# A gated mix of two attentions, forward and backward: preparation reordered, output projection of the first attention back in a stage of its own

## The chip, the core and the metric

The kernel runs on one core of a Trainium2 chip. The metric is device time in microseconds from start to end of one execution; the median of the runs is given. The engines are TensorE (PE, with its weight loads as PEld), VectorE (DVE), ScalarE (ACT), GpSimd (POOL) and SyncE (SP). SP and POOL issue nearly all DMAs.

## The reference

Inputs are bf16. The forward function and its vector-Jacobian product for 11 inputs are computed, so the kernel writes twelve outputs: the result and eleven gradients. With 2048 tokens and model width 576:

```python
g = _sigmoid((x * gate_w).sum(-1, keepdims=True))
a = _A_ref(x, A_wq, A_wk, A_wv, A_wo)      # 32 heads of 18, one shared k and v, no mask
b = _B_ref(x, B_mem0, B_Wq, B_Wk, B_Wv, B_Wo, 32)
return g * a + (1 - g) * b

def _B_ref(x, mem0, Wq, Wk, Wv, Wo, seg_len):   # 32 heads of 128
    mem = mem0                                   # 8 memory rows
    for s in range(64):                          # segments of 32 tokens
        h = concatenate([mem, xs])               # 40 rows
        q, k, v = projections of h
        p = softmax(where(mask, q k / sqrt(128), -1e9))
        o = (p v) Wo
        mem = o[:, :8]                           # carried to the next segment
        outs.append(o[:, 8:])
```

The memory rows make the second attention (B) a recurrence of 64 steps, forward and backward. The first (A) has no recurrence.

## The kernel before, in words

`build_full` (L1630) runs one stage after another; each opens pools of SBUF and PSUM memory, stacked in the order of the `with` lines, and the next stage's pools take the same addresses.

- Preparation: `prep` (L1173) loads x and grad_out, computes the gate g, transposes x into xT, makes g times grad_out (daT, da_dram) and (1-g) times grad_out (dbT, db_dram). `a_weights` (L1227) loads and lays out the weights of A, `a_setup` (L1265) makes k and v of A. `a_qd_all` (L1318) computes, in 16 head pairs times 4 blocks of 512 tokens, the transposed q and gradient products of A (`a_qd`, L1323): ten matmuls into one PSUM tile a_pq, their absolute values on ACT, one more matmul with a_smneg that adds a bound for the softmax, a copy by DVE, a store. `zero_fill` (L112) writes zeros to pq_dram (16 stores of 512 KB) and to the padding of otok_dram.
- Projections of B: `load_Wo`, `make_WoT` (L448) transposes Wo on PE; `b_proj_x` (L183) projects the 16 token tiles of dbT with WoT (dO). It also carries `stash_WT` (L177), 48 pieces: a transposing DMA of a piece of Wq, Wk or Wv into one of two p_wt buffers (SP), and its store to st_WT (POOL). Then `load_W` (L160) loads Wk, Wq and Wv (4.7 MB each), and `b_proj_x` projects five tiles of x with Wk, Wv and Wq; the other tokens' rows ride along in the chain.
- Forward chain: `b_chain_fwd` (L235), 64 segments, woven piece by piece (`weave`) with `a_pass1` (L1339), the forward softmax of A. Each segment also writes its heads' outputs, as oTm_dram and, copied into another order by POOL, as oh_dram (`head_out`). `a_pass1` ends with 128 small stores of a_dlT on SP. A's outputs go to otok_dram (L1456).
- Bulk stage: `b_bulk` (L473) does all token rows of attention B, forward and the larger part of backward, in 128 steps of four heads. Its ten to thirteen stage functions are called in a hand-written order (L697), each on another step, as a software pipeline: q, k and dO transposes, scores and exponentials (st_S), row sums and normalised P (st_R), transposes of P (st_T), output (st_O), its transposes (st_OT), gradient of the scores (st_D), b (st_B), transposes of dS (st_DT), dq (st_Q), memory gradients (st_K). Six of them share two PSUM buffers, x_tr.
- Backward chain (`b_chain_bwd`, woven with `a_pass2`), `b_post` (L930), and the weight gradients `b_dw` (L1042): 16 pieces of matmul groups, beside them the memory tokens of dq, dk and dv (`mem_tok`, L417), and per piece one tile of the gate (`gate_load`, `gate`, L720 to 754). `gate` does the output projection of A there: a transposing DMA of otok_dram, ten matmuls with w_wo, then the mix with b. For the memory rows of "o", `b_dw` reads oh_dram with transposing DMAs (L1057).
- `a_final` (L1556): the remaining gradients of A.

What orders the work: the four woven or pipelined stages stand under `manual_schedule`, where every engine's and queue's order is the program's. All other stages are ordered at compile time by the framework's planner, which takes any instruction whose inputs and memory are free in its own model of time, the earlier in the program first. [...]

Of the kernel before, what the change touches and what calls it, by code (L numbers as in the profile page):

```python
# [11 lines left out]
P = 128  # L12

D = 576
# [16 lines left out]
class Kern:  # L31
# [52 lines left out]
    def setup_B_dram(self, dram):  # L84
# [5 lines left out]
        self.da_dram = t("da_dram", [T, D])  # L90
        self.dxB_dram = t("dxB_dram", [T, D])
# [7 lines left out]
        self.oh_dram = t("oh_dram", [NSEG // 16, E, HB, P])  # L99
# [11 lines left out]

    def zero_fill(self, sp):  # L112
        nc = self.nc
        z = sp.tile([P, 16, P], BF16, name="zfill")
        nc.gpsimd.memset(z[:], 0.0)
        for tt in range(self.NTT):
            nc.gpsimd.dma_start(self.pq_dram[tt].rearrange("s q c w k -> (s q c) w k"), z[:])
        nc.gpsimd.dma_start(self.otok_dram[:, D:NKT * P].rearrange("(n p) d -> p n d", p=P), z[:, 0:self.NTT, 0:64])
# [41 lines left out]
    def load_W(self, pool):  # L160
        nc = self.nc
        self.W = {}
        for w, src in (("k", self.B_Wk), ("q", self.B_Wq), ("v", self.B_Wv)):
            t = pool.tile([P, NKT, J], BF16, name="W" + w)
            nc.vector.memset(t[64:128, 4, :], 0.0)
            for kt in range(NKT):
                rows = KT_ROWS[kt]
                self.dq_eng().dma_start(t[0:rows, kt, :], src[kt * P:kt * P + rows, :])
            self.W[w] = t
# [65 lines left out]
    def b_chain_fwd(self, keep, sp, psum):  # L235
# [33 lines left out]
        for s in range(NSEG):  # L269
# [8 lines left out]
            def head_out():  # L278
                c0 = 8 * (s % 16)
                nc.sync.dma_start(self.oh_dram[s // 16][:, :, c0:c0 + 8], oh[:].rearrange("p c u q -> p (c u) q"))  # L280

# [18 lines left out]
            for j in range(2):  # L300
                proj("k", j)
                if j == 0 and s + 1 < NSEG:
                    load_ride(s + 1)
                yield
# [54 lines left out]
            oh = sp.tile([P, 4, 8, 8], BF16, name="c_oh", bufs=1)  # L359
            nc.gpsimd.tensor_copy(oh[:], oT[:].rearrange("p u c q -> p c u q"))  # L360
            yield
            if s + 1 < NSEG:
# [13 lines left out]
                head_out()  # L376
# [18 lines left out]
            else:  # L395
                yield
                head_out()
# [19 lines left out]
    def mem_tok(self, wi, sp, psum, nb):  # L417
        nc = self.nc

        def load(mt):  # L420
            src = sp.tile([P, 16, 256], BF16, name="z_src", bufs=2)
            nc.sync.dma_start(src[:], self.dTm_dram[mt][:, wi])
# [50 lines left out]
    def b_bulk(self, wp, sp, psum):  # L473
# [76 lines left out]
        def transp(x, m, nm):  # L550
# [3 lines left out]
            self.tr(pt[:, 4, :], m.rearrange("p i t -> p (i t)"), P)  # L554
# [14 lines left out]
        def trans(t, w, nb):  # L569
            tt, g, r, d = view(t)  # L570
            pt = psum.tile([P, 5, P], BF16, name="x_tr", bufs=2)
            for i in range(4):
                self.tr(pt[:, i, :], d[w][:, 4 * (g % 4) + i, :], P)
            o = sp.tile([P, 4, P], BF16, name=f"x_{w}T", bufs=nb)
            self.evac(o[:], pt[:, 0:4, :], use="s" if w == "dO" else "v")
            sc[w + "T", t] = o

        st_QT = lambda t: trans(t, "q", 2)
        st_KT = lambda t: trans(t, "k", 2)
        st_GT = lambda t: trans(t, "dO", 6)  # L580

        def st_S(t):
# [13 lines left out]
            sc["E", t] = Et  # L596

        def st_R(t):
            tt, g, r, d = view(t)
            Et = sc.pop(("E", t))  # L600
# [80 lines left out]
        def st_K(t):  # L681
# [9 lines left out]
            if t % 4 == 3:  # L691
                c2 = t // 4 % 2
                for i in range(4):
# [3 lines left out]
        order = [(0, st_QT), (1, st_S), (2, st_T), (3, st_O), (0, st_KT), (1, st_R), (4, st_OT), (5, st_D), (0, st_GT),  # L697
                 (6, st_B), (7, st_DT), (8, st_Q), (6, st_K)]
        issue = (st_O, st_D, st_K, st_Q)
        with self.tc.manual_schedule():  # L700
# [8 lines left out]
            for t in range(NG + 8):  # L709
                for n, st in order:  # L710
                    if 0 <= t - n < NG:
                        st(t - n)
                    if st in issue and n in after and t - n >= 0 and (t - n) % 4 == 3:
# [6 lines left out]
    def gate_load(self, tt, sp):  # L720
        r = slice(tt * P, (tt + 1) * P)
        L = []
        for nm, src, dt in (("o_b", self.b_dram, F32), ("o_go", self.grad_out, BF16)):
# [3 lines left out]
        t = sp.tile([P, NKT, P], BF16, name="o_T", bufs=1)  # L727
        self.nc.sync.dma_start_transpose(t[:], self.otok_dram[r, :])
        L.append(t)
        return L  # L730

    def gate(self, tt, L, wo, sp, psum):
        nc = self.nc
        bsb, go, oT = L
        diff = sp.tile([P, D], F32, name="o_diff", bufs=1)
        pa = [psum.tile([P, 512], F32, name="w_acc", bufs=6) for _ in range(2)]
        for kt in range(NKT):
            for hf in range(2):
                self.mm(pa[hf][:, 0:288], lhsT=oT[:, kt, :], rhs=wo[:, kt, 288 * hf:288 * hf + 288],
                        start=(kt == 0), stop=(kt == NKT - 1))  # L740
        for hf in range(2):
            r = slice(288 * hf, 288 * hf + 288)
            nc.vector.tensor_tensor(out=diff[:, r], in0=pa[hf][:, 0:288], in1=bsb[:, r], op=ALU.subtract)
# [186 lines left out]
    def b_post(self, keep, sp, psum):  # L930
# [87 lines left out]
        with self.tc.manual_schedule():  # L1018
            for hc in range(3):
                if hc < 2:  # L1020
# [3 lines left out]
            hist = [self.hist_to_dram(a, b, sp, psum, "y_pt", 2)  # L1024
                    for a, b in ((self.dmT_dram, self.dm_dram), (self.memT_dram, self.mem_dram))]
            for t in range(NG + len(stages) - 1):
                if t % 8 == 7:
                    next(hist[t // 64 % 2], None)
# [13 lines left out]
    def b_dw(self, sp, psum):  # L1042
# [5 lines left out]
        def load(k):  # L1048
            which, jp = WS[k // 4], k % 4
            ts = []  # L1050
            for jc in (2 * jp, 2 * jp + 1):
# [3 lines left out]
                if k < 4:  # L1055
                    for mt in range(self.NM // P):
                        nc.sync.dma_start_transpose(  # L1057
                            t[:, NTT + mt, :].rearrange("p (h e) -> p h e", e=E),
                            self.oh_dram[mt][:, 4 * jc:4 * jc + 4, :].rearrange("e h t -> e (h t)"))
                else:  # L1060
# [698 lines left out]
```

## Time and profile before

| what | value |
|---|---|
| median of 3 runs | 6664.91 us (6661.47 to 6668.15) |
| the profiled execution's own time | 6664.91 us |
| its span, first to last instruction | 6663.0 us |
| mean granted TensorE clock | 0.968 |
| PE busy | 6031.6 us (91%) |
| DVE busy | 3991.9 us (60%) |
| ACT busy | 3371.7 us (51%) |
| POOL busy | 1737.6 us (26%) |
| DMA packets; moved | 1355820; 991.93 MB |

Stages by their first and last PE instructions: preparation to 226.9 us, WoT to 255, projection dO to 445, projections k, v, q 479 to 641, forward chain 655 to 2620, bulk 2683 to 3393, backward chain 3408 to 5236, b_post to 5824, weight gradients 5846 to 6530, a_final 6573 to 6663.

How to read it: the numbers are from one execution. A group of instructions is named by its line, engine, operation and "output <- inputs". Most matmuls have the line of a helper (L66, transposes L71), so tiles tell them apart. A wait is put down to the instruction or DMA that ended it. "SPq" is SP's issuing of DMAs.

### The profile page before, as it was taken

To read this page: it belongs to the slowest core of one execution; us is meant where nothing else is said; L and a number is where in the kernel's file an instruction comes from. 1 tells how busy PE (TensorE), PEld (TensorE's weight loads), DVE (VectorE), ACT (ScalarE), POOL (GpSimd) and SP (SyncE) were. 2 spreads that over 40 slices of the span, in tenths; PEclk is the share of its full clock that TensorE was granted. 3 is DMA by queue.
4 is the path that set the end of the run, shared out by engine and by line. 5 is a ranking of instruction groups with operands and counts; after the bars stand their busy time and mean duration, and the time that the engine had idled before them with its cause. 6 is when DMAs were issued, how large, how long until landed. Compare 5 with 4: busy or idle time off the path is not lost. (4 is left out here: it accounts for less than half of the span.)

```text
span 6663.0 us, 208545 instructions
## 1 busy us (share of the span) xinstructions
PE 6031.6 (91%) x88610; PEld 3351.1 (50%) x88822; DVE 3991.9 (60%) x7701; ACT 3371.7 (51%) x4849; POOL 1737.6 (26%) x3204
## 2 busy tenths in 40 slices
PE   6857999999999997899969999999999899989997
PEld 3323444444444443677844444444444577765443
DVE  4312788888888885566648888888888411111111
ACT  2212666666666665566646666666666322211100
POOL 3110232323232323444422222222222211112212
PEclk9978999999999998899989999999999999999998
DMA  5674444444444442899973434444434699896653
GB/s 183 193 233 142 88 93 93 94 94 93 93 93 95 91 92 62 243 256 258 260 252 98 101 100 102 96 103 97 101 99 100 173 238 246 218 284 206 220 163 109
DMA packets 1355820, 991.93 MB, mean 149 GB/s; under 512 B 928541, under 2 KB 1169446, under 8 KB 1344198
## 3 DMA queue, kind: packets, MB, share of 16 engines
q1 hardware_dynamic: 1268646, 759.03, 46.9%
q0 software_dynamic: 86240, 219.55, 9.7%
q8 instruction: 696, 11.40, 0.7%
q14 instruction: 238, 1.95, 0.1%
HBM read 552.41 MB, written 384.76 MB: 141 GB/s over the span
## 5 line engine op out<-in xcount | busy, mean ns | idle before, releaser
L1391 DVE TENSOR_TENSOR a_W<-a_dP,a_E 128x512 bf16<-128x512 f32 x2048 | 1311.4, 682 | 315.4 <-PE a_dP L66 253.8
L1522 DVE TENSOR_TENSOR b_dS<-b_dP,b_E 128x512 bf16<-128x512 f32 x2048 | 1314.8, 683 | 286.0 <-PE b_dP L66 205.3
L1501 ACT ACTIVATE b_E<-b_S 128x1024 bf16<-128x1024 f32 x1024 | 1047.9, 1023 | 554.9 <-PE b_dP L66 371.2
L1361 ACT ACTIVATE a_E<-a_S 128x1024 bf16<-128x1024 f32 x1024 | 1050.7, 1026 | 246.2 <-PE a_dP L66 142.0
L66 PE MATMUL b_dP<-b_KV,b_QD 32*128 32x512 bf16 x2048 | 601.7, 381 | 17.2 <-DVE b_dS L1522 17.1
L66 PE MATMUL a_dP<-a_QD,l_KV 32*128 32x512 bf16 x2048 | 503.3, 381 | 15.2 <-DVE a_W L1391 15.0
L66 PE MATMUL b_S<-b_KV,b_QD 32*128 32x512 bf16 x2048 | 400.1, 383 | 101.6 <-ACT b_E L1501 52.3
L66 PE MATMUL w_acc<-w_d,w_h 128*128 128x512 bf16 (+1 forms) x2352 | 470.9, 379 | 2.5
L66 PE MATMUL r_pj<-WT,r_dT 128*32 128x288 bf16 x12288 | 447.0, 288 | 0.0
L66 PE MATMUL a_S<-a_QD,l_KV 32*128 32x512 bf16 x2048 | 398.5, 383 | 47.0 <-ACT a_E L1361 42.9
L66 PE MATMUL a_acc<-a_W,l_WK 128*32 128x512 bf16 x4096 | 409.7, 390 | 0.1
L66 PE MATMUL b_acc<-b_dS,b_SD 128*32 128x512 bf16 x2048 | 404.7, 391 | 0.0
L66 PE MATMUL b_acc<-b_E,b_SD 128*32 128x512 bf16 x2048 | 404.3, 391 | 0.0
L66 PE MATMUL a_acc<-a_E,l_VK 128*32 128x512 bf16 x4096 | 398.7, 379 | 0.0
L998 DVE COPY y_T<-y_pt 128x512 bf16<-128x512 bf16 x256 | 97.0, 419 | 465.3 <-PE y_pt L71 465.3
L66 PEld LDWEIGHTS <-r_dT 128*32 128x32 bf16 x12288 | 330.7, 97 | 78.7 <-issue 0.9
L66 PEld LDWEIGHTS <-w_h 128*128 128x128 bf16 (+1 forms) x2400 | 213.0, 100 | 244.6 <-issue 3.4
L66 PEld LDWEIGHTS <-b_SD 128*32 128x32 bf16 x4096 | 105.2, 93 | 449.9 <-issue 448.8
L66 PEld LDWEIGHTS <-hm 128*32 128x32 bf16 x7680 | 209.9, 97 | 225.4 <-issue 15.5
L66 PEld LDWEIGHTS <-b_QD 32*128 32x128 bf16 x4096 | 140.4, 91 | 305.1 <-issue 214.6
L66 PEld LDWEIGHTS <-l_WK 128*32 128x32 bf16 x4096 | 105.2, 92 | 353.0 <-issue 352.9
L66 PE MATMUL y_pdx<-WT,y_T 128*128 128x288 bf16 x2048 | 272.2, 286 | 0.0
(419 smaller groups left out, 11374.4 us busy)
## 6 DMA issues: line engine op xcount, KB each, us to landing
b_QD<-qd_dram SPq DMA_DIRECT2D x256, 128.0 KB
b_SD<-sd_dram SPq DMA_DIRECT2D x256, 128.0 KB
dOx_dram<-p_tok SPq DMA_DIRECT2D x16, 1024.0 KB
c_vx<-vx_dram SPq DMA_DIRECT2D x256, 64.0 KB
krow_dram<-c_k POOLq DMA_DIRECT2D x64, 256.0 KB, 2.3
qrow_dram<-c_q POOLq DMA_DIRECT2D x64, 256.0 KB, 5.1
vrow_dram<-c_v POOLq DMA_DIRECT2D x64, 256.0 KB, 3.1
x_q<-qx_dram SPq DMA_DIRECT2D x32, 512.0 KB
```

Of the source, the lines that this page charges most:

```text
L66: return self.nc.tensor.matmul(out, lhsT, rhs, start=start, stop=stop, tile_position=tp, skip_group_check=True)
L998: nc.vector.tensor_copy(T_[t][w][:], pt[:])
L1361: nc.scalar.activation(E_[n][:], S.pop(n)[:], ACT.Exp, scale=SCALEA)
L1391: nc.vector.tensor_tensor(out=W_[n][:, i, :], in0=dP[i][:], in1=E_[n][:, i, :], op=ALU.mult)
L1501: nc.scalar.activation(E_[n][:], S.pop(n)[:], ACT.Exp, scale=SCALEA)
L1522: nc.vector.tensor_tensor(out=D_[n][:, i, :], in0=dP[i][:], in1=E_[n][:, i, :], op=ALU.mult)
```

## The change

- `a_weights` is called ahead of `prep`, in pools that are opened outside prep's; its PSUM tile a_wtr has two buffers.
- `a_qd_all` is pipelined by one block: the absolute values (now of all 128 rows) of a block are followed by the smneg matmul, copy and store of the block before. a_smneg has 128 rows, the lower 64 zero.
- `zero_fill` is gone. In each segment of the chain POOL writes a quarter of a tile of pq_dram (128 KB) from a constant of zeros.
- Wk and Wv have a pool of their own and are loaded ahead of the dO projection; Wq is loaded after it.
- oh_dram, its copy and its store are gone from the chain. After the chain, a new stage `a_out` loads otok_dram, transposes it on PE, multiplies by A_wo and writes a_dram; `b_mem_fwd` makes the memory tokens of "o" with `mem_tok(3)` and writes one of the two histories that `b_post` made.
- In `b_bulk` the three transposes of st_QT, st_KT and st_GT are one stage again at the front, st_R is part of st_S, the masks' transposes go in four pieces of 32 rows, and x_qT and x_kT have three buffers.
- `gate` reads a_dram in place of projecting; `b_dw` reads "o" of the memory rows like the others.

```diff
+    W = {}
+    def load_W(self, pool, ws):
...
     b_chain_fwd:
-            def head_out():
-                c0 = 8 * (s % 16)
-                nc.sync.dma_start(self.oh_dram[s // 16][:, :, c0:c0 + 8], oh[:].rearrange("p c u q -> p (c u) q"))
...
+                if j == 0:
+                    if s + 1 < NSEG:
+                        load_ride(s + 1)
+                    nc.gpsimd.dma_start(self.pq_dram[s // 4].rearrange("s q c w k -> (s q c) w k")
+                                        [:, 4 * (s % 4):4 * (s % 4) + 4, :], self.zeros[:].unsqueeze(1).to_broadcast([P, 4, P]))
...
-            oh = sp.tile([P, 4, 8, 8], BF16, name="c_oh", bufs=1)
-            nc.gpsimd.tensor_copy(oh[:], oT[:].rearrange("p u c q -> p c u q"))
...
     b_bulk:
-            self.tr(pt[:, 4, :], m.rearrange("p i t -> p (i t)"), P)
+            for i in range(4):
+                self.tr(pt[32 * i:32 * i + 32, 4, :], m[:, i, :], P, tp=(0, 32 * i))
...
+        def st_QT(t):
             tt, g, r, d = view(t)
+            for w, nb in (("q", 3), ("k", 3), ("dO", 6)):
+                pt = psum.tile([P, 5, P], BF16, name="x_tr", bufs=2)
+                for i in range(4):
+                    self.tr(pt[:, i, :], d[w][:, 4 * (g % 4) + i, :], P)
+                o = sp.tile([P, 4, P], BF16, name=f"x_{w}T", bufs=nb)
+                self.evac(o[:], pt[:, 0:4, :], use="s" if w == "dO" else "v")
+                sc[w + "T", t] = o
...
-        order = [(0, st_QT), (1, st_S), (2, st_T), (3, st_O), (0, st_KT), (1, st_R), (4, st_OT), (5, st_D), (0, st_GT),
-                 (6, st_B), (7, st_DT), (8, st_Q), (6, st_K)]
+        stages = (st_QT, st_S, st_T, st_O, st_OT, st_D, st_B, st_DT, st_Q)
+        order = list(enumerate(stages)) + [(6, st_K)]
...
     gate:
-        for kt in range(NKT):
-            for hf in range(2):
-                self.mm(pa[hf][:, 0:288], lhsT=oT[:, kt, :], rhs=wo[:, kt, 288 * hf:288 * hf + 288],
-                        start=(kt == 0), stop=(kt == NKT - 1))
+        nc.vector.tensor_tensor(out=diff[:], in0=at[:], in1=bsb[:], op=ALU.subtract)
...
+    def b_mem_fwd(self, sp, psum):
+        for gen in (self.hist_to_dram(self.memT_dram, self.mem_dram, sp, psum, "z_pt", 2), self.mem_tok(3, sp, psum, 2)):
+            for _ in gen:
+                pass
...
     a_qd_all:
+                absq = sp.tile([P, 512], BF16, name="a_absq", bufs=2)
+                self.nc.scalar.activation(absq[:, :], pq[:, :], ACT.Abs)
+                if prev is not None:
+                    self.a_qd_end(*prev, sp)
+                prev = (p, qb, pq, absq)
+        self.a_qd_end(*prev, sp)
...
+    def a_out(self, keep, sp, psum):
+        nc = self.nc
+        T, NTT = self.T, self.NTT
+        wo = keep.tile([P, NKT, D], BF16, name="o_wo")
+        for kt in range(NKT):
+            rows = KT_ROWS[kt]
+            nc.sync.dma_start(wo[0:rows, kt, :], self.A_wo[kt * P:kt * P + rows, :])
+        for tt in range(NTT):
+            trows = slice(tt * P, (tt + 1) * P)
+            ot = sp.tile([P, D], BF16, name="o_ot", bufs=3)
+            nc.sync.dma_start(ot[:], self.otok_dram[trows, :])
+            oT = self.tok_T(ot, sp, psum, "o")
+            pa = psum.tile([P, 640], F32, name="o_pa", bufs=2)
+            self.row_mm(pa, [(oT[0:KT_ROWS[kt], kt, :], wo[0:KT_ROWS[kt], kt, :]) for kt in range(NKT)])
+            a16 = sp.tile([P, D], BF16, name="o_a16", bufs=2)
+            self.evac(a16[:, :], pa[:, 0:D])
+            nc.gpsimd.dma_start(self.a_dram[trows, :], a16[:, :])
...
     build_full:
-        with SB("xk") as xk:
+        with SB("xk") as xk, SB("a1k") as a1k, SB("a1s") as a1s:
             with SB("p0s") as p0s, PS("p0ps") as p0ps:
+                k.a_weights(a1k, a1s, p0ps)
                 k.prep(cpool, xk, p0s, p0ps)
-            with SB("a1k") as a1k, SB("a1s") as a1s, PS("a1p") as a1p:
-                k.a_weights(a1k, a1s, a1p)
+            with PS("a1p") as a1p:
                 k.a_setup(a1k, a1s, a1p)
                 k.a_qd_all(a1s, a1p)
-                k.zero_fill(a1s)
-        with SB("bwo") as bwo:
+        with SB("bwo") as bwo, SB("bw1") as bw1:
             k.load_Wo(bwo)
             with SB("bwt") as bwt, SB("pds") as pds:
                 with PS("wop") as wop:
                     k.make_WoT(bwt, wop)
+                k.load_W(bw1, ("k", "v"))
                 with PS("pdp") as pdp:
                     k.b_proj_x(("dO",), k.dbT_dram, pds, pdp, k.NTT)
-            with SB("bw") as bw:
-                k.load_W(bw)
+            with SB("bw2") as bw2:
+                k.load_W(bw2, ("q",))
...
+        with SB("aok") as aok, SB("aos") as aos, PS("aop") as aop:
+            k.a_out(aok, aos, aop)
+            k.b_mem_fwd(aos, aop)
         with SB("xw") as xw, SB("xs") as xs, PS("xp") as xp:
             k.b_bulk(xw, xs, xp)
```

## The prediction

> **What bounds the kernel now.** I read the page's forty slices first, then a table of stages (columns: stretch, length, busy time and instructions of PE, PEld, DVE, ACT, POOL, granted clock, DMA share, GB/s), then the waits inside each stage that the change touches.
>
> ```profile
> 104.00:226.00 122.00, 103.31 (x746) 39.76 (x744) 47.61 (x73) 39.78 (x69) 23.23 (x42) 1.00 0.38 135
> 226.00:255.00 29.00, 13.82 (x161) 12.37 (x160) 10.82 (x22) 11.37 (x21) 3.45 (x5) 0.65 1.04 337
> 255.00:480.00 225.00, 149.04 (x628) 65.04 (x642) 46.05 (x67) 34.89 (x64) 28.56 (x53) 0.85 0.79 221
> 480.00:641.00 161.00, 136.06 (x586) 60.06 (x598) 41.72 (x61) 34.34 (x59) 0.00 (x0) 0.89 0.46 170
> 641.00:2620.00 1979.00, 1897.20 (x34005) 886.86 (x34003) 1581.53 (x2942) 1347.42 (x1790) 589.39 (x1311) 0.99 0.46 91
> 2620.00:2683.00 63.00, 2.88 (x20) 2.04 (x19) 0.57 (x3) 2.31 (x4) 8.09 (x15) 0.50 0.21 61
> 2683.00:3393.00 710.00, 658.66 (x9849) 551.14 (x9976) 455.19 (x1040) 429.76 (x910) 321.84 (x384) 0.97 0.92 257
> ...
> 5824.00:6530.00 706.00, 672.66 (x4207) 380.07 (x4256) 118.37 (x236) 68.62 (x110) 141.18 (x227) 0.98 0.67 209
> ```
>
> The forward chain (641 to 2620), the bulk stage (2683 to 3393) and the weight gradients (5824 to 6530) are PE-bound, the bulk stage with its DMA queues at 0.92 as well. Up to 641 PE is not the bound: 149 busy us in 225 for the first projection (dO). Waits there (waiter, who ends the wait: total us, times, longest), of SP's queue and then of the engines:
>
> ```profile
> SPq L180 <- DMA st_WT<-p_wt: 110.8, 42, 4.5
> ```
> ```profile
> DVE p_tok L61 <- DMA dOx_dram<-p_tok: 111.6, 11, 16.0
> ...
> DVE Wk L165 <- DMA st_WT<-p_wt: 29.2, 1, 29.2
> ```
> SP issues the 48 transposing loads of stash_WT (L180), and each waits until one of two p_wt buffers has been stored. The projection's own store (L200) stands behind them in SP's order, so PE follows the stash and not its matmuls; the weights wait for the stash's last store too. In the q/d stage PE waits once per block for the absolute values:
>
> ```profile
> PE a_pq L66 <- ACT a_absq L1333: 14.6, 48, 0.3
> ```
> Between chain and bulk, 128 small stores of a_dlT hold ACT, PE and SP:
>
> ```profile
> ACT a_dlT L1415 <- DMA qd_dram<-a_dlT: 32.4, 3, 11.1
> PE x_tr L71 <- DMA x_q<-qx_dram: 25.4, 1, 25.4
> ```
> One line of SP's timeline (start, us, what) matters more than its size:
>
> ```profile
> 40.36 0.97 SPq L190 DMA_DIRECT2D p_x<-xT_dram  x2
> ```
> These loads belong to the second projection, which starts at 479. Outside hand-ordered blocks the planner thus lifts a DMA to wherever its pool's memory is free. The opposite case: the stash's first load goes at 236.3, just when the last q/d store (issued 227.9, 7.8 us to landing) frees memory under its pool.
>
> [...] Wk, Wq and Wv were issued on both queues within 5 us of 474 and kept the share near 1.0 for some 45 us. [...] four 128x32 matmuls of x_m start 0.07 us before the next four[...]. [...]
>
> **Part by part.**
>
> 1. *q/d products.* A block takes 1.87 us (starts 140.51, 142.38): five pairs of matmuls at 0.215, then the wait, then the smneg matmul at 0.30. With the smneg of the block before, PE has 5 x 0.215 + 0.30 = 1.37. Abs on 128 rows costs as on 64 (0.59), the copy 0.69, the store lands in 2.1 with three buffers: all under 1.37. 64 blocks from 110.5 to 226.9 are 1.82 each, so 64 x 0.45 = **-29**.
>
> 2. *Weights first* (and two a_wtr buffers). From 72.5 (prep's last transpose) to 110.5 (first smneg) PE waits for memory release, weights, copies. Afterwards KV (5 us), abs (1.9), reduce (2.3), scale and start remain, some 11; but 15 small loads at 0.43 on SP and about 13 us of POOL work (wo issues 2.7, wkv copies 7, memset 4.4) now stand ahead of x and grad_out, making prep some 8 to 10 longer: 38 - 11 - 9 = **-18**. The ten DVE copies move with it into DVE's idle start.
>
> 3. *Zero blocks.* The 16 stores at 98.9 to 131.4 are hidden under q/d now: 0 gained. In the chain one POOL issue of about 0.54 per segment is added and the 0.41 copy and SP's 0.60 store of oh are removed; none is in PE's waits. **0**, -5 to +5.
>
> 4. *Stash and the two weights.* The pool pds of the stash now begins above 36 + 80 + 40 = 156 KB (bwo, bw1, bwt by their tile shapes); the preparation's pools end at 40 + 29.7 + 20.3 + 62.9 = 153 KB. So nothing holds the stash, and by the p_x line the planner will lift it to the start. It is then on SP and POOL, ahead of the stores of da, db and q/d in both queues, behind which DVE waits for its three d16 and three QDs buffers. It goes at its own pace: 4.68 us each in before (322.8 to 393.0, 15 steps). Without it stage 1 would end at 226.9 - 29 - 18 = 180; with it, at 48 x 4.5 + 3 plus a tail of 10 = **229** (48 x 4.0 gives 200; a mutual stall as in dO, 250). I take 229: the saving of parts 1 and 2 is spent on hiding the stash. Then WoN and make_WoT 24 (29 before, with stash traffic): 253. dO at PE's pace, 16 x 8.63 + 1 = 139: 392. Wk and Wv load under it (9.4 MB, about 28 us of full DMA in 139). The next p_x waits for the last 1 MB store of the pool beneath, +8: 400. 15 x 8.63 = 130: 530. Wq is needed 17 us in; at 4.7 MB and near 400 GB/s it takes 13. Before, the last matmul was at 641: -111, less 2 for Wq: **-109** for parts 1 to 4, from -145 to -60.
>
> 5. *Output projection as a stage of its own (a_out), memory tokens, history.* PSUM of these stages lies over c_x, which ACT reads last at 2668.7. Per tile PE has 5 transposes (0.3) and 10 matmuls (5 x 0.216 + 5 x 0.05): 1.65, x16 = 26; mem_tok 128 x 0.055 = 7; history 1. The loads from the fourth tile on stand behind the last 32 a_dlT stores (to 2678). End about 2708, last store landed 2714. The masks and the four x_mB memsets, hidden at 2606 to 2622 today, lie over this memory: 13 us, then the vB load 3: first x_po at 2731 against 2692.6: **+38**. Waits behind POOL's memsets: SP's vB, then vT and chunk 1. If loads and PSUM come earlier, +15; at 2.5 us a tile, +60.
>
> 6. *Bulk order.* An undisturbed step is 4.83 (x_q transposes at 2999 to 3003.41, PE full); the mean is 5.46 (91.5 steps in 500), the rest waits for stores (DVE x_dS 30, POOL x_P 26, ACT x_o 18 us in 500). Now q, k, dO transposes come back to back through two x_tr buffers: dO waits for q's copy (result 0.44, copy 0.42): 0.90 instead of 0.44. S follows; dO's copy, E (0.60 + 0.27) end at 2.84; the reduce now stands at once behind it: 0.81 + 0.22, PT 0.50, dS 0.68, dSm 0.28 on DVE: 5.4; st_K needs x_m free: 5.47 + 0.24 = **5.7**. PE itself has 4.83 + 0.46 + two times 0.07 to 0.15 for the split transposes = 5.5. DMA needs 0.93 x 5.46 = 5.1. I take 5.8: 128 x 0.35 = **+45**; 5.55 gives +12, 6.1 +80.
>
> 7. *Weight gradients.* 160 matmuls of 288 columns leave: at 0.1225, **-19.6**; 20 history transposes -1. The transposing loads of oh (SP 13.5 us at the start) become plain: -4 (0 to -12). The gate's a load and its one subtraction from SBUF lie on POOL and DVE, which are idle there. **-25**.
>
> Sum: -109 + 0 + 38 + 45 - 25 = **-51**. The profiled execution took 6664.91 (span 6663.0, 1.9 around it), which is the median too: **6614**.
>
> **Rivals.** *The stash stays with dO* (planner or memory differs): only -29 - 18 and some 18 of loads under dO: -65 + 38 + 45 - 25 = -7, 6658. Against it: the p_x line. *Slower: the stalls for stores add to the longer bulk step* instead of hiding in it: 5.7 + 0.63 = 6.33, 128 x 0.87 = +111, so -109 + 38 + 111 - 25 = +15, 6680; it decides from 6.31 us a step. For it: waits and chain fall on DVE both. Against: a longer step leaves the DMA 10% slack. *Everything hides*: q/d end 195, a_out +15, bulk +15: -143 + 15 + 15 - 28 = -141, 6524.
>
> **How the numbers follow.** Forecast 0.60 (own range 6575 to 6650), stash stays 0.14 (6640 to 6675), slower 0.16, everything hides 0.10. About 0.2% (13 us) is what a measurement of this kernel can tell from no change. Faster: 0.57 + 0.06 + 0.10 + 0.01 = 0.74; same 0.13; slower 0.13. The range 6550 to 6672 leaves out most of the last two cases.
>
> **What would show it.** Right: transposing loads of p_wt before 30 us; q/d blocks without the abs wait; dO tiles every 8.6 us; first chain matmul near 545; a PE-thin stretch of about 100 us between chain and bulk, ending near the first x_po; bulk steps of 5.7 to 5.9 with DVE's reduce ahead of x_PT; no w_wo rows. Wrong: q/d ending beyond 260 because SP and POOL stall on the stash; a bulk step near 5.4 or beyond 6.3; a_out already running under the a_dlT stores.

## The result, and the profile after

The change made the kernel slower, by about half a per cent. The median went from 6663.2 us (4 runs, 6658.6 to 6668.2) to 6693.4 us (4 runs, 6685.3 to 6707.2); the ratio is 1.0047, 95% interval 1.0025 to 1.0069. The prediction was 6614. The profiled execution of the changed kernel, at 6707.2 us (span 6705.4), is the slowest of its four; a second profile of it, from the experiments below, has a span of 6676.7. Both stand in this table, cut at the first and last matmuls of each stage (us). The prediction puts the first x_po at 2692.6, which is the transpose of x_Pm ahead of it; here the first x_po matmul is meant, 2696.4 in the kernel before.

| stretch | before | after | after, second profile | forecast |
|---|---|---|---|---|
| to the first chain matmul | 655.2 | 566.3 | 565.2 | -109 |
| forward chain | 1965.1 | 1982.6 | 1968.8 | 0 |
| last chain transpose to first x_po | 76.1 | 144.6 | 143.4 | +38 |
| bulk, first to last x_po | 698.2 | 762.4 | 761.4 | +45 |
| to the backward chain | 13.3 | 13.7 | 13.8 | 0 |
| backward chain | 1815.7 | 1829.9 | 1832.2 | 0 |
| b_post, with its edges | 622.9 | 611.3 | 600.0 | 0 |
| weight gradients | 683.6 | 660.5 | 659.0 | -25 |
| to the end | 132.9 | 134.1 | 132.9 | 0 |
| span | 6663.0 | 6705.4 | 6676.7 | -51 |

Each column adds up to its span. Two more profiles of the kernel before (below) show how far one execution can be trusted: they reach the first chain matmul at 650.0 and 651.4, and take 615.4 and 617.1 us for b_post; in every other stretch they lie within 4 us of the first. First the table of stages of the changed kernel, which answers to the one shown of before (stretch, length, busy us and instructions of PE, PEld, DVE, ACT, POOL, granted clock, DMA share, GB/s).

```profile
91.00:226.00 135.00, 94.76 (x760) 57.91 (x759) 48.04 (x75) 40.10 (x69) 34.82 (x64) 0.97 0.85 220
226.00:254.00 28.00, 13.12 (x160) 11.60 (x161) 11.76 (x23) 11.04 (x20) 5.20 (x9) 0.68 1.05 389
254.00:400.00 146.00, 139.47 (x627) 62.85 (x640) 44.49 (x65) 37.22 (x64) 2.63 (x5) 0.99 0.56 201
400.00:552.00 152.00, 131.62 (x588) 59.28 (x600) 42.72 (x61) 34.66 (x60) 0.60 (x2) 0.92 0.38 140
...
2549.00:2668.00 119.00, 56.54 (x401) 31.46 (x404) 24.73 (x46) 21.22 (x36) 24.68 (x38) 0.67 0.36 120
2668.00:2693.00 25.00, 10.37 (x90) 8.29 (x90) 5.86 (x14) 4.12 (x9) 16.71 (x45) 0.50 0.30 76
2693.00:3456.00 763.00, 689.38 (x10540) 545.12 (x10663) 438.38 (x1027) 410.57 (x903) 318.56 (x380) 0.98 0.85 240
5910.00:6572.00 662.00, 652.17 (x4048) 363.66 (x4096) 116.10 (x221) 68.72 (x110) 146.11 (x237) 0.99 0.61 212
```

The first projection (third line) is now nearly all PE, 139 of 146 us, where it was 149 of 225. The q/d stage (first line) hardly ends earlier: its last matmul ends at 221.5, where it was 226.9, and PE is busy for 95 of 135 us. Chain to bulk (fifth and sixth lines) has become 144 us at half a PE or less. The bulk's DMA share fell from 0.92 to 0.85: it is longer, and waits less for transfers.

The stash went where the prediction put it: its first load, in SP's timeline, stands at 11.89 us.

```profile
11.89 7.04 SPq L174 DMA_TRANSPOSE p_wt<-in_B_Wq_dram  x1
```

In the waits of SP's own queue up to 560 us, the stash's wait for its stores has halved (110.8 before):

```profile
SPq L174 <- DMA st_WT<-p_wt: 52.9, 22, 5.1
```

In the engines' waits of the q/d stage (91 to 226 us) the wait for the absolute values is gone, and another is there in its place: DVE can't write the next q/d block until a store of an earlier one has landed, and PE waits for DVE.

```profile
DVE a_QDs L1305 <- DMA qd_dram<-a_QDs: 65.0, 31, 4.1
...
PE a_pq L66 <- DVE a_QDs L1305: 34.6, 29, 2.7
```

The second projection starts late. In the timeline its first x tile is issued 10 us after the last dO matmul of 398.6, and lands 10 us later still. It is issued when the last dO store has landed (8.0 us of waiting in SP's queue), and Wq's 4.7 MB, issued from 399.0 on, are ahead of it; over 399.0 to 419.4 us the DMA share is 0.99 and 307 GB/s are moved:

```profile
409.62 3.57 SPq L184 DMA_DIRECT2D p_x<-xT_dram  x3
...
419.45 1.01 PE L66 MATMUL p_pb<-Wk,p_x 128*128 128x512 bf16 x2 [20.49 <-DMA p_x<-xT_dram]
```

Between chain and bulk, lines of the timeline (the bracket has the engine's idle time before, and who ended it):

```profile
2592.72 0.58 ACT L1384 COPY a_dlT<-c_x 64x512 bf16<-64x512 bf16 x1 [10.47 <-DMA qd_dram<-a_dlT]
...
2609.80 0.42 DVE L401 COPY h_mtk<-z_pt 128x512 bf16<-128x512 bf16 x1 [4.70 <-DMA mem_dram<-h_mtk]
...
2618.80 0.40 PE L71 MATMUL z_pt<-identB,z_v 128*128 128x128 bf16 x2 [2.62 <-DVE z_v L422]
2618.99 0.31 PE L71 MATMUL o_ptr<-identB,o_ot 128*128 128x128 bf16 x1
...
2664.89 1.01 ACT L63 COPY z_tk<-z_pt 128x1024 bf16<-128x1024 bf16 x1 [6.08 <-DMA om_dram<-z_tk]
...
2679.37 0.58 PE L66 MATMUL x_S<-maskX,identB 128*128 128x512 bf16 x1 [7.51 <-POOL maskM L476]
```

The output projection starts at 2593, when the last a_dlT copy frees PSUM, as forecast. Then history and memory tokens stand between its tiles in PE's order: they wait for a store (4.70), for DVE's copy of z_v (2.62), and o_ptr waits behind them; no o_pa matmul runs from 2603.3 to 2621.5. After the last tile (2655.7) the tokens go on to 2668, with a wait of 6.08 for a store; then come the bulk's masks.

### The profile page after: what moved, and what is told of

Read it like the earlier page. It is cut to its first block, busy times and chain, and to the rows that moved or that the text cites. A ratio compares the mean times of both kernels' runs of the same rounds, so it can differ in the third digit from the quotient of the medians.

```text
span 6705.4 us, 210417 instructions
## 1 busy us (share of the span) xinstructions
PE 6094.1 (91%) x89583; PEld 3384.5 (50%) x89798; DVE 3986.1 (59%) x7720; ACT 3389.3 (51%) x4881; POOL 1765.9 (26%) x3224
```

## The experiments

Medians of the kernel before on the same chips were 6657 to 6659. "Below" and "above" mean differences of medians, unless a profile is named.

**again.** The changed kernel, no edit.

> The changed kernel once more, unchanged, for a second profile. Theory (clock): the two recurrent chains were longer in the profiled execution (forward 1983 us against 1965 of the kernel before, backward 1843 against 1828) only because that execution was granted a lower clock (0.99 where before had 1.00, 0.97 where it had 0.98); in an execution near 6685 us the forward chain takes 1965 to 1972 and the backward one 1828 to 1834. Rival (zero blocks): the 64 stores of zeros that now stand in POOL's order of the forward chain really lengthen it, so it takes 1980 or more in every execution. Either way the time is 6685 to 6707.

6677.9 us (ratio 1.0031, 1.0016 to 1.0045). The forward chain took 1968.8 us. So 14 of the 17 us that the first profile has there over the kernel before belong to that execution and not to the change, and go with its clock: by the trace's clock records it had 53.6 us at half clock in the forward chain, this one 30.7, before 26.6. (Such counts, here and below, include some 10 us just ahead of a chain's first matmul.) An estimate from these: if half clock costs half its time, the 22.9 us between the two make 11 of the 14. Part 3's zero is right. The backward chain stayed at 1832, against expectation; see before_again.

**bulk_old.** The bulk functions of the kernel before, in the changed kernel.

```diff
-        stages = (st_QT, st_S, st_T, st_O, st_OT, st_D, st_B, st_DT, st_Q)
-        order = list(enumerate(stages)) + [(6, st_K)]
+        order = [(0, st_QT), (1, st_S), (2, st_T), (3, st_O), (0, st_KT), (1, st_R), (4, st_OT), (5, st_D), (0, st_GT),
+                 (6, st_B), (7, st_DT), (8, st_Q), (6, st_K)]
...
-            for i in range(4):
-                self.tr(pt[32 * i:32 * i + 32, 4, :], m[:, i, :], P, tp=(0, 32 * i))
+            self.tr(pt[:, 4, :], m.rearrange("p i t -> p (i t)"), P)
```

> The changed kernel with the bulk stage of the kernel before: its order, its single transposes of x_m. Theory: the new order costs 132 starts of (5.79 - 5.32) us, so the bulk falls from 763 to about 702 us between its first and last x_po and the time by 60, to 6630 to 6640, faster than before. Rival: the old order's stalls for stores get worse because the stage now starts with other transfers under way, and only 20 to 30 us come back (6660 to 6675).

6623.3 us (0.9950, 0.9934 to 0.9966), 55 below again; its bulk takes 699.4 us against 761.4. The theory holds: without the bulk's part the change is a gain of 34 us on before.

**reduce_late.** Only the reduce and what follows it goes back to a step of its own.

```diff
+            sc["E", t] = Et
+
+        def st_R(t):
+            tt, g, r, d = view(t)
+            Et = sc.pop(("E", t))
             l = sp.tile([P, 4], F32, name="x_l", bufs=2)
...
+        order.insert(4, (1, st_R))
```

> The changed kernel with one part of the old bulk order: the sum over x_E (the reduce), its reciprocal and the two products of x_P are a step of their own again, behind st_O instead of straight behind the two exponentials; the three transposes stay together. Theory (the reduce is ahead of x_PT on VectorE): 0.81 + 0.18 us leave the loop that sets the step, and it falls from 5.79 to 5.0 to 5.4, -50 to -100 us. Rival (the three transposes back to back through two x_tr buffers set the loop): the step stays between 5.6 and 5.8, at most -25 us.

6677.1 us (1.0030, 1.0019 to 1.0042), 1 below again. The theory falls: starts of x_S lie 5.79 us apart, as before the edit (smallest 5.78, largest 5.79, in 85 steps). VectorE's order was not what set the step.

**single_tr.** Only the split transposes are undone.

```diff
-            for i in range(4):
-                self.tr(pt[32 * i:32 * i + 32, 4, :], m[:, i, :], P, tp=(0, 32 * i))
+            self.tr(pt[:, 4, :], m.rearrange("p i t -> p (i t)"), P)
```

> The changed kernel with only the split transposes of the bulk stage undone: x_Pm and x_dSm are transposed in one piece of 128 columns again, not in four of 32; the order of the step stays new. Theory: the step of 5.79 us is TensorE's own queue, and the split pieces take 0.41 us of it (x_P and x_dS 0.31 us instead of 0.22 to the next start, x_Pm and x_dSm 0.17 instead of 0.06); 132 starts x 0.41 = 54, so about 6620 to 6630, with a step of 5.38, or a little above if stalls for stores come back at that pace. Rival: the three transposes back to back, with their wait of 0.45 us for x_qT's copy, set the step; it stays above 5.65 and at most 18 us come back (6660 or more).

6633.2 us (0.9963, 0.9950 to 0.9976), 45 below again; by the profiles the bulk takes 710.3 us against 761.4, and the median step is 5.35 (mean 5.41). The theory holds. The rows are in PE's timeline; the start of the next matmul says what a group took. Before (first profile):

```profile
2999.27 0.38 PE L71 MATMUL x_tr<-identB,x_P 128*128 128x128 bf16 x4
2999.49 0.22 PE L71 MATMUL x_tr<-identB,x_Pm 128*128 128x128 bf16 x1
2999.55 0.38 PE L66 MATMUL x_po<-x_vmB,x_PT 128*128 128x512 bf16 x1
```

The changed kernel, second profile:

```profile
3045.40 0.38 PE L71 MATMUL x_tr<-identB,x_dO 128*128 128x128 bf16 x4 [0.29 <-DVE x_qT L61]
...
3046.22 0.38 PE L71 MATMUL x_tr<-identB,x_P 128*128 128x128 bf16 x4
3046.54 0.24 PE L71 MATMUL x_tr<-identB,x_Pm 128*32 128x128 bf16 x4
3046.71 0.39 PE L66 MATMUL x_po<-x_vmB,x_PT 128*128 128x512 bf16 x1
```

single_tr:

```profile
3044.35 0.38 PE L71 MATMUL x_tr<-identB,x_P 128*128 128x128 bf16 x4
3044.57 0.22 PE L71 MATMUL x_tr<-identB,x_Pm 128*128 128x128 bf16 x1
3044.63 0.38 PE L66 MATMUL x_po<-x_vmB,x_PT 128*128 128x512 bf16 x1
```

From x_P to x_po it is 0.28 in one piece (2999.27 to 2999.55, 3044.35 to 3044.63) and 0.49 in four (3046.22 to 3046.71). The same happens at x_dS and x_dSm: 0.41 a step. The instruction's own duration (0.24 against 0.22) shows nothing of it. The timeline of the weight loads (PEld) shows where it goes, in the changed kernel's second profile:

```profile
3046.22 0.21 PEld L71 LDWEIGHTS <-x_P 128*128 128x128 bf16 x3
3046.53 0.10 PEld L71 LDWEIGHTS <-x_Pm 128*32 128x32 bf16 x4
3046.70 0.11 PEld L66 LDWEIGHTS <-x_PT 128*128 128x128 bf16 x2
```

The four pieces start within 0.01 us of each other. But the load of the first comes 0.15 us after the start of the last x_P matmul (3046.39), and that of x_PT, in full width again, 0.16 us after the last piece. In one piece both loads follow at once, and the next matmul starts 0.055 us after the one before. So the price is paid on the way into a group of 32-column pieces and out of it. The groups of x_m pay it too: 0.15 and 0.20 us in single_tr (3047.58 to 3047.73, 3047.82 to 3048.02).

The [0.29] at x_dO is the wait of the three transposes together. It is still there in single_tr, whose step is 5.35 where the old order has 5.08 undisturbed (median of 90 steps; the mean, with its stalls for stores, is 5.47). That the wait alone makes this difference was not tested: the reduce and the buffers differ as well.

**out_old.** Output projection, tokens and history as in the kernel before; preparation and bulk as changed. (Here, in prep_only and in the three kernels built on it, the 64 zero columns that the gate's transposing loads read are written by one store ahead of q/d.)

```diff
-        with SB("aok") as aok, SB("aos") as aos, PS("aop") as aop:
-            k.a_out(aok, aos, aop)
-            k.b_mem_fwd(aos, aop)
...
-                self.gate(k, gl, sp)
+                self.gate(k, gl, wo, sp, psum)
```

> The changed kernel with the output projection, the memory's output tokens and the history back where the kernel before has them (products in the weight gradients, transposing loads of oh_dram, history in b_post). Theory: the stretch from the last transpose of the forward chain to the first x_po falls from 144 to about 72 us, the weight gradients give back 24 and b_post 10: -38, about 6655. Rival (the stretch is held by something else than the new stage, say by the a_dlT stores and the masks): -72 does not come, the kernel gets slower by 15 to 35 us, 6705 to 6725.

6648.6 us (0.9989, 0.9982 to 0.9996), 29 below again. By the profiles the stretch from chain to x_po is 78.0 against 143.4 (-65), the bulk 747.7 against 761.4 (-14), weight gradients 682.4 against 659.0 (+23), b_post 17 longer. The theory holds, with one more term: behind the late stage the bulk also starts slowly. In its first 110 us PE is busy for 82 us in again and 95 here. In the waits of these 110 us one accounts for the difference, a load that is not yet in; first again, then out_old:

```profile
PE x_tr L71 <- DMA x_q<-qx_dram: 19.9, 1, 19.9
```
```profile
PE x_tr L71 <- DMA x_q<-qx_dram: 6.4, 1, 6.4
```

**mem_old.** The output projection stays a stage of its own; tokens and history go back.

```diff
             k.a_out(aok, aos, aop)
-            k.b_mem_fwd(aos, aop)
...
+                if k < 4:
+                    for mt in range(self.NM // P):
+                        nc.sync.dma_start_transpose(
```

> The changed kernel with the memory's output tokens and the history back as in the kernel before (transposing loads of oh_dram, history in b_post), but the output projection still as a stage of its own. It splits the stretch between forward chain and bulk. Theory: the tokens and the history take about 20 of the 65 us that this stretch gained (12 after the last o_pa matmul, the rest between its tiles), so the stretch falls from 143 to about 123 us from the last chain transpose to the first x_po; b_post gives back 17 and the loads of oh_dram 0 to 4: near the changed kernel's 6678, 6665 to 6685. Rival: the tokens hide under the output projection's waits for loads, at most 8 us come back, and the time rises to 6685 to 6700.

6626.8 us (0.9954, 0.9939 to 0.9969), 51 below again, which neither side expected. The stretch fell to 111.7 us, by 31.7 where 20 was expected. Of the rest, 26 lie in the backward chain, which this edit doesn't touch: 1805.9 us, with 57.9 us at half clock instead of 102.4 (see before_again). The tables of the two kernels, first mem_old, then again (a_dlT stores; output projection; masks):

```profile
2537.00:2580.00 43.00, 3.62 (x25) 2.38 (x23) 0.62 (x4) 2.90 (x5) 3.91 (x11) 0.52 0.04 10
2580.00:2624.00 44.00, 38.73 (x226) 16.45 (x229) 10.55 (x23) 10.66 (x23) 8.20 (x15) 0.85 0.50 156
```
```profile
2534.00:2579.00 45.00, 3.53 (x29) 2.45 (x26) 1.11 (x3) 2.62 (x5) 6.08 (x12) 0.51 0.17 56
2579.00:2652.00 73.00, 52.70 (x381) 28.45 (x379) 24.22 (x43) 18.51 (x32) 18.58 (x26) 0.78 0.47 162
```

Alone, the sixteen tiles take 44 us with PE busy for 39; with tokens and history 73, with PE busy for 53. The extra 14 us of PE are half of the extra 29 us, and more than the 8 that were forecast: at the lower clock (0.78 against 0.85) many transposes of the tokens start 0.107 us apart instead of 0.055. The rest is waiting. Also, b_post is as short as in again (556 us, first to last y_pk) though both histories are back in it: the moved history is not why it became shorter.

**prep_only.** The kernel before with the preparation's part of the change alone. The two new calls in the schedule are:

```diff
             with SB("p0s") as p0s, PS("p0ps") as p0ps:
+                k.a_weights(a1k, a1s, p0ps)
...
+                k.load_W(bw1, ("k", "v"))
...
-                k.load_W(bw)
+                k.load_W(bw2, ("q",))
```

> The kernel before with the preparation's part of the change alone: weights first, q/d products pipelined by one, zero blocks in the chain, Wk and Wv loaded under the first projection. Output projection, bulk order and history are as before. Theory: the 90 us that the changed kernel is ahead at the first chain matmul stay to the end, nothing after it is worse: before - 85 to - 95, about 6565 to 6575. Rival: part of them is given back later, [...]: - 40 to - 60, 6600 to 6620.

6593.6 us (0.9904, 0.9889 to 0.9918): 65 below before, between theory and rival. Against the first profile of before it has -85 at the first x_po (2611.6) and -80 at the last; then 16 are lost in the backward chain (1831.3 us, 85.3 at half clock). Elsewhere nothing more is given back. It beats both kernels.

**stash_plain.** prep_only with plain loads for the transposing ones. It leaves out the transposition of Wq, Wk and Wv for the backward chain, and what depends on it is not computed.

```diff
-        self.nc.sync.dma_start_transpose(t[:], src[:, 256 * j:256 * j + 256])
+        self.nc.sync.dma_start(t[:].rearrange("p a d -> p (a d)"),
+                               src.rearrange("d j -> (d j)")[147456 * j:147456 * (j + 1)].rearrange("(p x) -> p x", p=P))
```

> The kernel with the preparation's part alone, and in it the 48 transposing loads of the stash of weights replaced by plain loads of the same bytes (rows of 2304 bytes); the stashed weights are then not the transposed ones, so the transposition of Wq, Wk and Wv is left out and what depends on it is not computed. Theory: the transposing loads' own pace (48 x some 4.4 us = 211 us from the start) sets the end of the q/d products at 225 and slows the first tiles of the first projection; with plain loads q/d ends at 180 to 195 and the chain starts 40 to 50 us earlier than with the transposing ones. Rival: the q/d stage is held by its own stores, or by preparation that grew longer, not by the stash; it ends within 10 us of 225.

6582.2 us (0.9885, 0.9868 to 0.9901). The last a_pq matmul is at 209.7 instead of 225.0, and the chain starts 17 us earlier: neither theory, but between them. Transposing costs 15 us of the stage; most of the stash's price there stays when the loads are plain.

**qd_act.** prep_only with the q/d stores on ScalarE's queue.

```diff
-        (nc.sync if qb % 2 == 0 else nc.gpsimd).dma_start(self.qd_dram[p][:, qb * 512:(qb + 1) * 512], QD[:, :])
+        nc.scalar.dma_start(self.qd_dram[p][:, qb * 512:(qb + 1) * 512], QD[:, :])
```

> The kernel with the preparation's part alone, with one edit: the 64 stores of q/d products leave from ScalarE's queue instead of SP's and POOL's, where the stash's loads and stores stand. Theory (order in the queues): the q/d stores waited behind stash instructions that wait for p_wt; without that q/d ends at 185 to 200 instead of 225, and the stash's remaining pieces slow the first projection by some 10 to 20 us at most, so the chain starts 10 to 30 us earlier than 569.6. Rival (the transfers themselves are slow beside the transposing ones, whatever queue issued them): q/d ends at 215 or later, no gain.

6588.4 us (0.9898, 0.9881 to 0.9914); the last a_pq matmul is at 223.9 and the chain starts at 582.7, later than in prep_only. DVE's wait for q/d stores fell from 58.7 to 8.8 us and the stage was no shorter; 41 us of ACT's idle time before the absolute values are now put down to loads of the stash. Order in SP's and POOL's queues is then not the whole reason, but the edit puts stores between ScalarE's absolute values, so it is not a clean test.

**spread.** prep_only with the stash taken out of preparation and q/d: 24 pieces under each projection in a hand-written order, and the second projection's x tiles in memory of their own, loaded ahead of Wq.

```diff
+        with self.tc.manual_schedule():
...
+                    for c in range(c0 + (c1 - c0) * i // n, c0 + (c1 - c0) * (i + 1) // n):
+                        self.stash_WT(c, sp)
...
+                    xs = [k.proj_load(k.xT_dram, i) for i in range(2)]
+                    k.load_W(bw2, ("q",))
```

> The kernel with the preparation's part alone, and the stash spread by a hand-written order: 24 pieces under the first projection (1.5 a tile), 24 under the second, none under preparation and q/d; the second projection's x tiles lie in memory of their own and are loaded ahead of Wq. Theory: 1.5 x 4.5 us = 6.75 us of transposing loads fit beside the 8.63 us of a tile, so q/d ends near 185, the first projection takes 140, the second 130 without its wait of 20 us for p_x, and the chain starts near 495 to 510 instead of 568: about 60 us below the kernel with the preparation alone, near 6510. Rival: transposing loads in SP's queue hold up the projection's stores whatever their number, tiles take 12 us, the chain starts at 560 or later, no gain.

6498.7 us (0.9759, 0.9745 to 0.9774): 95 below prep_only, 160 below before, the best of the study; the theory holds. Its table (q/d; WoT; first projection; second):

```profile
87.00:176.00 89.00, 86.52 (x744) 66.30 (x744) 48.28 (x72) 39.02 (x69) 18.00 (x34) 1.00 0.35 112
176.00:208.00 32.00, 13.65 (x161) 11.68 (x161) 12.42 (x24) 11.04 (x20) 4.83 (x8) 0.68 1.02 386
208.00:347.00 139.00, 138.30 (x641) 62.57 (x641) 43.93 (x65) 37.15 (x64) 11.78 (x22) 1.00 0.94 273
347.00:481.00 134.00, 131.51 (x600) 59.05 (x600) 42.47 (x61) 34.47 (x60) 14.76 (x28) 0.99 0.89 263
```

The q/d stage and both projections are PE-bound. q/d ends 49 us earlier than with the stash beside it (last smneg matmul at 175.9 against 225.0 in prep_only; 8 of these are gained in preparation, whose last transpose is at 76.4 instead of 84.4), both projections run at 8.63 to 8.9 us a tile with transposing loads under them, and the second starts 1.1 us after the first (345.9, 347.0).

**before_again, before_again2.** The kernel before, no edit.

> The kernel before, unchanged, for a second profile of its chains. Theory (execution, not change): its backward chain also takes 1828 to 1837 us in an execution with some 85 to 100 us at half clock in it, and the 1816 of the first profile is one end of a scatter. Rival: 1816 with about 65 us at half clock every time; then the changed kernel's backward chain really pays some 14 us for a clock that it is granted less of.

> The kernel before, unchanged, a third profile of its chains, as above: 1828 to 1837 us in the backward chain in at least one of the two by the theory, 1816 in both by the rival.

6646.2 and 6659.8 us. The backward chain took 1815.0 and 1818.7 us, with 61.4 and 71.7 us at half clock; the first profile had 1815.7 and 64.9. The theory falls as far as these go: three executions of before lie at 61 to 72 us, two of the changed kernel at 99.0 and 102.4.

But the clock is not all. A step of the backward chain, from one first matmul of r_pj with WoT to the next, has a median of 27.61 us in the three profiles of before and of 27.96 in the two of the changed kernel. Near the end of the longer steps DVE starts one product late, and PE waits for it. Two neighbouring steps of the changed kernel, the first of 27.96 us, the second of 27.60:

```profile
4292.11 1.29 DVE L1491 TENSOR_TENSOR b_dS<-b_dP,b_E 128x512 bf16<-128x512 f32 x2 [0.56 <-PE b_dP L66]
...
4319.71 1.29 DVE L1491 TENSOR_TENSOR b_dS<-b_dP,b_E 128x512 bf16<-128x512 f32 x2 [0.21 <-PE b_dP L66]
```

From the fourth step on, DVE is idle for over 0.45 us at this place in 30 of 61 steps in both profiles of the changed kernel, and in 1 of 61 in each profile of before. The b_dP matmul named there had long ended, so what holds DVE is not in the trace. An estimate: 30 times 0.35 us are 10 of the 14 to 17 us. The half clock stands close by: of its single periods of 3.4 us, 10 of 13 and 9 of 14 begin in the changed kernel within 0.5 us of the border between two steps, just behind this place; all ten in the three profiles of before begin 11 us into a step. In the timeline of the first profile each of its 10 begins 1.6 to 2.2 us behind the start of a late b_dS (gap of 0.56 or 0.58). So in time the lower clock comes behind the late start; whether one brings about the other no run shows.

The code of this stage is the same in all kernels, and their 14 profiles fall into two groups: those of before, mem_old, qd_act and spread have the late start in 0 or 1 of 61 steps, all others in 27 to 31. prep_only and qd_act differ only in the queue of the q/d stores, more than 3 ms earlier. The chip alone does not explain it: single_tr, prep_only and stash_plain (27 to 30) ran on the same one as spread (1).

## Why the prediction was wrong, step by step

No single step carries the miss. Against the span of before the second profile has +13.7 where -51 was forecast, 65 apart: part 5 is 29 of it, part 4 19, part 6 18 (14 of them again the stage of part 5), and the backward chain, which the prediction left out of its sum without a reason, 16 (b_post, the forward chain and the edges, below, make up the difference).

1. **q/d products, and 2. weights first**: right where they can be seen. The absolute values take 0.597 us on 128 rows, 0.590 on 64 in the kernel before. Without the stash beside it (spread), q/d ends at 175.9; the two parts' sum gave 180. The first smneg matmul comes 18 us earlier (92.6 for 110.6; -18 forecast), and from it to the last it is 33 us less (-29 forecast).
3. **Zero blocks**: right; the forward chain takes 1963 to 1969 us in the nine profiles that have 24 to 31 us at half clock in it, against 1965 before with 27.
4. **Stash**: right in kind and in its first terms (q/d end 221.5 and 218.8 for 229, first dO matmul at 254 for 253, tiles at PE's pace). The pace it went by, 8.63 us a tile, is that of 40 matmuls of 128x512 in the second projection of before, between the stores at 624.82 and 633.45: 216 ns each. The part is **wrong by 19 to 20 in size**. "The next p_x waits for the last 1 MB store of the pool beneath, +8" was 20.5: the store took 10, and Wq's load, issued just ahead, another 10. The prediction priced Wq where it is used (2 us; 13 of loading at near 400 GB/s, where before had 388 from 232 to 236 us, but 337 over the loads of 474 to 519), and not where it is in the way; with x tiles in memory of their own and ahead of Wq the gap is 1.1 (spread, which takes both waits away together). The stash's last pieces cost dO 5 to 6 more (144.6 for 139).
5. **Output projection: the step that failed.** +38 became +67. "mem_tok 128 x 0.055 = 7; history 1" is the term: only PE's time was summed, at full clock, and the waits on DVE's and POOL's copies of z_v (1.9 each) and on single-buffered stores were left out. mem_old puts it at 31.7: 14 more of busy PE, the rest waits. The output projection itself, with the masks behind it, cost 35.6 (111.7 - 76.1), near the 30 that the other terms make; its tile took 2.2 (1.07 + 3.34 for two tiles, in the timeline) and not 1.65. The masks were rightly seen (25 us from x_tr to x_po).
6. **Bulk order: the step right by luck, its reasons wrong.** The step was put at 5.8 and is 5.79. But the reduce, the 5.4 to 5.7 of that step's working, costs nothing here (reduce_late). The split transposes, put at 0.14 to 0.30, cost 0.41: the 0.07 behind that is the distance between two groups of narrow pieces, and a group between full-width matmuls pays on the way in and out. The three transposes were put at 0.46 over an undisturbed step of 4.83. That step is misread: the x_q transposes start at 2998.33 and 3003.41, which makes 5.08, and single_tr is 0.27 above that. That PE's starts add up to 5.79 after all (5.08, 0.27 and, by the step, 0.44) is luck. The sum is +63 and not +45 mainly because of the slow start behind part 5's stage: without that stage (out_old) the bulk takes 747.7, +49.5.
7. **Weight gradients**: right, -24.6 for -25 (the other profiles of before have 682). mem_old splits it: 664.0 us without the gate's products, -19.6 as forecast, and 659.0 with the plain loads of the tokens too, -5 for -4.

**Not foreseen**: the backward chain, +16.5 (second profile), and b_post, -22.9 (-15 to -17 against the other profiles of before, -11.6 in the first profile of the changed kernel). The forward chain adds 4 to the 65, the remaining edges 1, and b_post takes 23 off. The slower rival named a mechanism that isn't there: the changed bulk has no stalls for stores at all, all but the first seven of its steps and the last lie within 0.02 us of each other.

What stays open: what makes DVE start late in the backward chain, and what the clock adds to that; why b_post is shorter in kernels with the output projection as a stage (it isn't the history), and how much of the stash's 49 us under q/d is queue order and how much its transfers. The tokens behind all sixteen tiles of the output projection, or its loads ahead of the a_dlT stores, were not tried.

## What to carry to other kernels

Price a new stage by the waits among its own engines, not by its busiest engine: the tokens, priced at 8 us of PE, took 32, because their buffers were single, PE's order put them ahead of ready work and the clock was lower there (0.78, without them 0.85). Splitting one wide transpose into four narrow ones on the engine that sets the step was paid here in the starts of its neighbours (0.21 us), hardly in its own duration (0.24 for 0.22): read start to start, and from a place with the same neighbours. And before hiding a bulk of transfers under a stage, look for one whose DMA share is low and whose own stores don't turn around small buffers: the 48 pieces of the stash cost preparation and q/d stage 49 us, 15 of them for transposing, and PE-bound projections next to nothing (8.63 to 8.9 us a tile in spread).

## What the runs showed of the hardware

- A transpose of 128 columns in four pieces of 32, into four partition ranges, cost 0.2 us more from start to start than in one piece (0.49 against 0.28 with the 4 transposes before it). The pieces themselves start within 0.01 us; the time goes into the change from full width to 32 columns (0.15 us to the next start instead of 0.055) and back (0.16). Two groups of narrow matmuls in a row, those of x_m, start only 0.07 us apart.
- Transposing transfers cost the stage that they share a little: replacing the 48 of the stash by plain loads shortened preparation and q/d by 15 us of 225 (last a_pq matmul at 209.7 in stash_plain, 225.0 in prep_only).
- The clock records of the backward chain hold, past the first 70 us, single periods of 3.4 us at half clock, 2 to 5 in three executions of before and 13 and 14 in two of the changed kernel, whose code there is the same. In the changed kernel's first profile the 13 periods begin on one grid of 3.41 us, and in the 3.41 us ahead of each PE is busy for 91 or 92% of the time, where the median of the grid's 515 stretches is 95.5%; but 169 of these have 91.6% or less, so PE's busy time as the trace has it does not tell where the half clock comes. Here, in mid-chain, the number of periods goes with the kernel more than with the run.
